# First hop in a bucket pass: gather and scatter runs of four and five without lag, and a PSUM bank moved from the lookup to the gather ring

## The chip, the cores and the metric

One NeuronCore of a Trainium2 chip runs the kernel. The metric is device time in microseconds of one execution. Names used below: TensorE is PE (its weight loads are PEld), VectorE is DVE, ScalarE is ACT, GpSimd is POOL, SyncE is SP, which issues most DMAs. PSUM has eight banks, and a tile here fills a bank or a part of one.

## The reference: what is computed

A graph of 10000 nodes with 160000 random edges and 128 features per node. Seven hops propagate the features over normalized edges; then a small attention block over the eight tokens of every node, and a readout.

```python
h = x
toks = [x]
for _ in range(K):                                   # K = 7
    msg = h[src] * deg_inv_sqrt[src, None] * deg_inv_sqrt[dst, None]
    h = _segment_sum(msg, dst, N)
    toks.append(h)
tok = jnp.stack(toks, axis=1)                        # (N, K+1, D)
t = _layernorm(tok, axis=-1)
...
o = tok + jnp.einsum('nkd,de->nke', o, wo)
...
return jnp.einsum('nk,nkd->nd', alpha, o)
```

## The kernel before, in words

**Stages.** `pass_a` and `decode` sort edges into cells; then comes the bucket pass, which this document is about; hops 2 to 7 follow; attention comes last. Nodes are cut into 79 tiles of 128. The bucket pass handles tiles in quads of four (20 of them), and does three things at once for three quads in a row, as three generators that a loop in `run` advances in turn, sixteen steps per quad:

- `place` (L419) sorts the edges of a quad, two tiles at a time. For each pair it counts keys (L431, 25 matmuls into the PSUM tile `ur`), evicts the counts to `H` (L432, ACT), forms offsets (L437) evicted to `U2` (L439, ACT), ranks by `ux` (L220, DVE) and 16 matmuls L224 and one L225 into `ur` again, reduces the ranks to `rk` (L228, DVE), makes one-hot rows and products `R` (L207, L213, DVE), and looks up with 50 matmuls (L450, 25 for each tile of the pair) into the PSUM tile `tb`, which ACT evicts to `tbs` (L451). `tb` has a bank of its own in the pool `psm`. At a quad's end two DMAs write `srow` and `drow`, small matmuls (L466, L468, L480, L499) make indices and the matrix `Sov` for edges that spill over; `ohp` (L495-L499) are DVE one-hots.
- `matrices` (L509) makes each tile's matrix `w` of gather and scatter one-hots: a row `rb` is loaded (L516), DVE compares it (L525), three matmuls L528 per tile write `x` (PSUM, from the same ring as the gathers, tag "p"), ACT turns `x` into one-hots (L529), DVE adds the rest (L533), and a DMA stores `w` (L535).
- `hop1` (L698) does the first hop for a quad with `block` (L549). A tile has nine gathers. A gather (`gather`, L603) is two passes of four matmuls L609, 32 columns of weights each, into a bank `p` of the ring `pg`; the evacuation to `eb`, one of five buffers, is by ACT (L614), and in the last quad by ACT and DVE in turn. Its scatter (`scat`, L576) is two pairs of matmuls L559 and L560, 128 columns of weights, from `eb` into the accumulator `acc` (two banks). Two fetched rows per tile (`og`, indirect DMAs on POOL, L545) are scattered in the same way; the last of them is in `close` (L589), which ends the tile and hands `acc` to `fin1` (L677: `indeg` on DVE, `y`, `r` and `tab` on ACT and DVE, stores on SP).

**The order in `block`.** `runs` says how many gathers are issued in a row, and `lag` how many scatters stay pending after each run; the rest are emitted behind the run. Then the generator yields. In the first hop runs are 2, 2, 2, 3 with a lag of two, so a scatter is always two gathers behind, and a tile takes four steps. `close` is pending as well, so it comes in the next tile's first run.

**Who orders the queues.** When the program is built, a scheduler sets each engine's order from the program's order, the dependences and its own costs; a queue is then strictly in order. Only attention is ordered by hand.

**PSUM in the bucket pass.** Eight banks: `ur` one, `tb` one, `msc` one, the ring `pg` three, `acc` two.

Of the kernel before, what the change touches and what calls it, by code (L numbers as in the profile page):

```python
# [7 lines left out]
F32 = mybir.dt.float32  # L8
# [7 lines left out]
PSUM = bass.MemoryType.PSUM  # L16
# [14 lines left out]
NS = 4 * NJ  # L31
# [9 lines left out]
class Hops:  # L41
# [377 lines left out]
    def place(self, ts, got):  # L419

        tc, nc, V, A, T, G = self.tc, self.nc, self.nc.vector, self.nc.scalar, self.nc.tensor, self.nc.gpsimd
# [3 lines left out]
        for p0 in range(0, n, 2):  # L425
            cols = lambda z: z[:, :, ts[0] + p0:ts[0] + p0 + 2]
            oh = self.onehot(wp, "oh", cols(self.kB), NS)
            ur = self.pU.tile([128, 512], F32, name="ur")
            H = wp.tile([128, NS, 2], F16, name="H")
            for c in range(NCH):  # L430
                T.matmul(ur[:, :2 * NS], self.id16, oh[:, c], start=c == 0, stop=c == NCH - 1)  # L431
            A.copy(H, ur[:, :2 * NS].rearrange("p (k i) -> p k i", i=2))  # L432
            yield
            U = ur[:, 512 - 2 * NS:].rearrange("p (k i) -> p k i", i=2)
            h = NS // 4
            for w in range(4):
                T.matmul(U[:, w * h:(w + 1) * h], self.triw[:, w, :], H[:, w * h:(w + 1) * h], start=True, stop=True)  # L437
            U2 = wp.tile([128, NS, 2], F16, name="U2")
            A.copy(U2, U)  # L439
            yield  # L440
            rk = self.rank(wp, w1, ur, oh, U2, cols(self.wB))
            ro = self.onehot(w1, "rob", rk, CAP)
            R = w1.tile([128, NCH, 2 * CAP, 2], F16, name="R")
            self.times(R[:, :, :CAP], ro, cols(self.sl))
            self.times(R[:, :, CAP:], ro, cols(self.dl))
            yield
            tb = self.psm.tile([NS, 2, 64], F32, name="tb")
            for g in range(2):
                for c in range(NCH):
                    T.matmul(tb[:, g, :], oh[:, c, :, g], R[:, c, :, g], start=c == 0, stop=c == NCH - 1)  # L450
            A.copy(tbs[:, p0:p0 + 2, :], tb)  # L451
            vo = wp.tile([128, NCH, 2], F32, name="vo")
            V.scalar_tensor_tensor(vo, rk, float(CAP), cols(self.TT), op0=ALU.is_ge, op1=ALU.mult)
            for g in range(2):
                V.max(ov[:, p0 + g, :], vo[:, :, g])
            yield
# [92 lines left out]
    def block(self, t, w, tab, og, pend, lag, runs, first, evac, fin, lead=False, late=False, mid=None, ahead=None,  # L549
              after=None):  # L550

        nc, V, A, T, G = self.nc, self.nc.vector, self.nc.scalar, self.nc.tensor, self.nc.gpsimd
        acc = []

        def both(W, rows, start, ones):

            T.matmul(acc[0][:, :128 + ones], W, rows[:, 128:256 + ones], start=start, stop=False, skip_group_check=True)  # L559
            T.matmul(acc[0][:, :128], W, rows[:, :128], start=False, stop=False, skip_group_check=True)  # L560


        def fetched(i, start=False, stop=False):
            W = w[:, (NG + i) * 128:(NG + i + 1) * 128] if i < NI else self.Sov[:, t, :]
            if first:
                both(W, og[i], False, 0)
                T.matmul(acc[0][:, 128:129], W, self.ones16, start=False, stop=stop, skip_group_check=True)  # L567
                return
            T.matmul(acc[0][:, :256], W, og[i], start=start, stop=stop)  # L569

        def begin():
            acc.append(self.pacc.tile([128, 512], F32, name="acc", tag="acc"))
            for i in range(NI if late else NI + 1):
                fetched(i, start=i == 0)

        def scat(e, jj):  # L576
            if not acc:
                acc.append(self.pacc.tile([128, 512], F32, name="acc", tag="acc"))
            for j in range(e.shape[1]):
                J = 2 * jj + j  # L580
                if first:
                    both(w[:, J * 128:(J + 1) * 128], e[:, j], J == 0, 1)
                else:
                    T.matmul(acc[0][:, :256], w[:, J * 128:(J + 1) * 128], e[:, j, :256], start=False, stop=J == NG - 1 and not late)  # L584
                if first and J == 0 and not lead:
                    for i in range(NI):
                        fetched(i)

        def close():  # L589
            if first:  # L590
                if lead:
                    for i in range(NI):
                        fetched(i)
                fetched(NI, stop=True)
                fin(t, acc[0][:, :128], acc[0])
                return
            if late:
                T.matmul(acc[0][:, :256], self.Sov[:, t, :], og[NI], start=False, stop=True)  # L598
            s = self.fp.tile([128, 128], F32, name="s")
            V.tensor_reduce(s, acc[0][:, 0:256].rearrange("p (h d) -> p d h", h=2), axis=X, op=ALU.add)  # L600
            fin(t, s, acc[0])

        def gather(jj):  # L603
            n = min(2, NG - 2 * jj)
            p = self.pg.tile([128, 2, 2, 128], F32, name="p")
            for j in range(n):
                for q in range(4):
                    s = 4 * (2 * jj + j) + q
                    T.matmul(p[32 * q:32 * q + 32, j], w[:, NJ * 128 + s * CAP:NJ * 128 + (s + 1) * CAP], tab[:, s, :], start=True, stop=True)  # L609
            e = self.ebuf[self.eb_i % len(self.ebuf)]  # L610
            self.eb_i += 1
            pv = p[:, :n].rearrange("p j h d -> p j (h d)")
            if evac(jj):
                A.copy(e[:, :n, 0:256], pv)  # L614
            else:
                V.tensor_tensor(e[:, :n, 0:256], pv, self.one[:, :, None].to_broadcast([128, n, 256]), op=ALU.mult)  # L616
            pend.append(lambda: scat(e[:, :n], jj))

        jj = 0
        for i, n in enumerate(runs):  # L620
            for _ in range(n):
                gather(jj)
                if jj == 0 and not first and not mid:
                    ahead(self.ebuf[(self.eb_i - 1) % len(self.ebuf)][:, 0, 0:1])
                jj += 1
            if mid:
                mid(0)
            if not first:
                begin()
                if mid:  # L630
                    ahead()
            while len(pend) > lag:
                pend.pop(0)()
            if mid:
                mid(1)
            if after:
                after()
            if i == len(runs) - 1:
                pend.append(close)
            yield  # L640
# [17 lines left out]
    def run(self, ctx, att, nhop=K):  # L658
        tc, nc, V, A, T, G = self.tc, self.nc, self.nc.vector, self.nc.scalar, self.nc.tensor, self.nc.gpsimd
        with ExitStack() as c:  # L660
# [3 lines left out]
            self.pass_a()  # L664
            self.decode()
            self.gsp = c.enter_context(tc.tile_pool(name="gs1", bufs=6))
            self.pg = c.enter_context(tc.tile_pool(name="pg1", bufs=3, space=PSUM))
            self.pacc = c.enter_context(tc.tile_pool(name="pc1", bufs=2, space=PSUM))
            self.ogp = c.enter_context(tc.tile_pool(name="og1", bufs=2))
            self.fp = c.enter_context(tc.tile_pool(name="fp1", bufs=1))  # L670
# [1 line left out]
            pend = []  # L672
# [25 lines left out]
            def hop1(q):  # L698
                for t, w in zip(quads[q], W[q]):
                    og = [self.fetch(t, j, (self.tabd[0], self.tabh[0])) for j in range(NI + 1)]  # L700
                    yield from self.block(t, w, self.tab[0], og, pend, 2, (2, 2, 2, 3), True,
                                          lambda jj: q < nq - 1 or jj % 2 == 0, fin1, t == quads[0][0])

            nq, last1 = len(quads), quads[-1][-1]
# [22 lines left out]
        with ExitStack() as c:  # L727
# [10 lines left out]
            pend = []  # L738
            for k in range(2, nhop + 1):
# [30 lines left out]
                og = [[None] * (NI + 1) for _ in order]  # L770
# [11 lines left out]
                for n, t in enumerate(order):  # L782
                    w = self.gsp.tile([128, (NJ + NG) * 128], F8, name="w")
# [546 lines left out]
```

## Time and profile before

| what | value |
|---|---|
| median of 3 runs | 3995.84 us (3982.39 to 4321.17) |
| profiled execution | 4027.3 us, its span 4025.2 us, mean granted TensorE clock 0.974 |
| sorting, until the bucket pass's first gather | 0 to 441 us |
| bucket pass | 441 to 1218 us |
| hops 2 to 7 | 1218 to 3342 us |
| attention | 3342 to 4025 us |

The stages' bounds are the first and last starts of their lines in the trace. The profiled execution is 31 us longer than the median. Busy time is the union of an engine's instructions; matmuls are pipelined and their ends are modelled, so a TensorE that is shown busy may still lose time between instructions, which is seen in their starts.

### The profile page before, as it was taken

How to read it: one execution, taken by the hardware profiler on the slowest of the kernel's cores; microseconds unless marked ns; L12 is line 12 of the kernel's file. 1: busy time of each engine (PE TensorE's matmuls, PEld its weight loads, DVE VectorE, ACT ScalarE, POOL GpSimd, SP SyncE). 2: the span in 40 equal slices, each digit the busy share in tenths (PEclk: the TensorE clock that was granted, in tenths of full speed). 3: DMA queues.
4: the chain of work that ended last, by engine and by line, in shares of the span. 5: the costliest groups of instructions: out<-in, count | busy, mean ns of one | idle time of the engine just before them, and what ended most of it. 6: DMA issues, size and time to landing. Idle time of an engine off the chain costs nothing.

```text
span 4025.2 us, 169111 instructions
## 1 busy us (share of the span) xinstructions
PE 3816.7 (95%) x71507; PEld 3075.5 (76%) x71507; DVE 3203.1 (80%) x6886; ACT 2847.4 (71%) x7067; POOL 1716.4 (43%) x2343
## 2 busy tenths in 40 slices
PE   6887899999999999999999999999999999999997
PEld 4665666667667888888888788888888887887885
DVE  8998777777757777777777777777776665999998
ACT  6884577777776666666666666666665667888884
POOL 0000222232335665666566566656656662222222
PEclk8998899999999999999999999999999999999998
DMA  3100444444455666666666666666666652222220
GB/s 105 31 2 1 146 149 142 146 150 149 149 172 161 198 202 192 202 200 201 193 198 203 188 207 202 200 190 201 202 192 200 187 186 84 74 73 73 78 79 13
DMA packets 326582, 595.67 MB, mean 148 GB/s; under 512 B 61559, under 2 KB 219477, under 8 KB 320565
## 3 DMA queue, kind: packets, MB, share of 16 engines
q1 hardware_dynamic: 287861, 507.11, 40.2%
q0 software_dynamic: 35392, 72.55, 6.4%
q8 instruction: 560, 9.18, 1.0%
q10 hardware_dynamic: 2560, 5.12, 0.4%
q14 instruction: 209, 1.71, 0.1%
HBM read 455.67 MB, written 128.91 MB: 145 GB/s over the span
## 4 chain that ended last, share of the span: by engine, by line
PE 71%; DVE 19%; DMA 5%; ACT 3%; issue 2%; SPq 0%; another core or an unknown queue 0%; DVEq 0%; POOL 0%; POOLq 0%; ACTq 0%
PE p L609 27%; PE acc L584 23%; PE acc L569 4%; DVE o L213 2%; DMA rb<-srow 2%; PE tb L450 2%; PE ur L224 2%; DVE st L1110 2%; DVE oh L207 2%; DVE ux L220 2%; PE acc L559 2%; PE pv L1004 1%; DVE tab L1021 1%; PE po L1015 1%; PE acc L560 1%
## 5 line engine op out<-in xcount | busy, mean ns | idle before, releaser
L614 ACT CAST eb<-p 128x512 f16<-128x512 f32 x3065 | 1623.0, 600 | 562.5 <-PE p L609 336.2
L616 DVE TENSOR_TENSOR eb<-p,one 128x512 f16<-128x512 f32 x1912 | 1232.0, 686 | 328.3 <-PE acc L584 183.6
L609 PE MATMUL p<-tab,w 128*32 128x256 f16 x39816 | 1296.6, 275 | 30.7 <-issue 15.3
L609 PEld LDWEIGHTS <-w 128*32 128x32 fp8e4 x39816 | 989.5, 96 | 233.1 <-issue 177.5
L584 PE MATMUL acc<-eb,w 128*128 128x256 f16 x8532 | 1013.2, 273 | 0.0
L584 PEld LDWEIGHTS <-w 128*128 128x128 fp8e4 x8532 | 836.5, 98 | 98.7
L545 POOL DMA_INDIRECT og<-tabh,oidx x553 | 607.4, 1098 | 675.8 <-DVE vi L490 389.1
L545 POOL DMA_INDIRECT og<-tabd,oidx x541 | 540.9, 1000 | 804.8 <-PE acc L567 453.2
L654 POOL TENSOR_SCALAR r<-s,ctok 128x128 f32<-128x128 f32 x474 | 294.8, 622 | 43.9 <-DVE s L600 27.1
L645 ACT ACTIVATE tab<-s,c 128x128 f16<-128x128 f32 x395 | 158.6, 401 | 206.6 <-DVE eb L616 178.3
L646 DVE SCALAR_TENSOR_TENSOR tab<-s,c,tab 128x128 f16<-128x128 f32 x395 | 138.9, 352 | 180.6 <-issue 169.7
L1029 ACT ACTIVATE junk<-tab 128x128 f32<-128x128 f32 x625 | 245.2, 394 | 0.0
L341 ACT ACTIVATE rs<-iof,rb 128x128 fp8e4<-128x128 f32 x784 | 231.8, 390 | 0.3
L559 PE MATMUL acc<-eb,w 128*128 128x129 f16 x1422 | 215.0, 223 | 1.3 <-ACT eb L614 1.3
L600 DVE TENSOR_REDUCE s<-acc 128x128 f32<-128x256 f32 x474 | 196.8, 415 | 20.2 <-PE acc L598 14.2
L560 PE MATMUL acc<-eb,w 128*128 128x128 f16 x1422 | 210.5, 221 | 0.0
L559 PEld LDWEIGHTS <-w 128*128 128x128 fp8e4 x1501 | 139.0, 98 | 75.9 <-issue 75.9
L529 ACT ACTIVATE w<-x,one 128x512 fp8e4<-128x512 f32 x237 | 149.2, 689 | 62.8 <-PE x L528 60.3
L1015 PEld LDWEIGHTS po<-v,pT 128*128 128x128 f32 x1250 | 159.6, 194 | 42.0 <-issue 27.6
L544 POOL COPY og<-eb 128x1 f16<-128x1 f16 x452 | 83.9, 186 | 250.4 <-ACT eb L614 250.4
L1004 PE MATMUL pv<-Wv,xT 128*128 128x131 f32 x1250 | 176.4, 284 | 1.6 <-ACT xT L984 1.1
L1087 POOL TENSOR_TENSOR p<-e,in 128x512 f32<-128x512 f32 (+1 forms) x40 | 40.8, 1021 | 320.1 <-DVE e L1085 320.1
(301 smaller groups left out, 5448.0 us busy)
## 6 DMA issues: line engine op xcount, KB each, us to landing
w<-gsd SPq DMA_DIRECT2D x474, 592.0 KB
gsd<-w SPq DMA_DIRECT2D x79, 592.0 KB
rb<-srow SPq DMA_DIRECT2D x79, 576.0 KB
tok<-r SPq DMA_DIRECT2D x546, 64.0 KB
tab<-tok SPq DMA_DIRECT2D x273, 128.0 KB
tabd<-tab SPq DMA_DIRECT2D x396, 64.0 KB
og<-tabh,oidx POOLq DMA_INDIRECT x553
og<-tabd,oidx POOLq DMA_INDIRECT x541
```

What stands on the lines that cost most here:

```text
L341: A.activation(ro[:, j - a, i, :], self.iof, AF.Abs_reciprocal_sqrt, scale=2.0 ** 21, bias=rb[:, j - VP, i:i + 1], saturate=False)
L545: self.nc.gpsimd.indirect_dma_start(out=o, out_offset=None, in_=src[0] if i == NI else src[1], in_offset=bass.IndirectOffsetOnAxis(ap=self ...
L559: T.matmul(acc[0][:, :128 + ones], W, rows[:, 128:256 + ones], start=start, stop=False, skip_group_check=True)
L560: T.matmul(acc[0][:, :128], W, rows[:, :128], start=False, stop=False, skip_group_check=True)
L584: T.matmul(acc[0][:, :256], w[:, J * 128:(J + 1) * 128], e[:, j, :256], start=False, stop=J == NG - 1 and not late)
L609: T.matmul(p[32 * q:32 * q + 32, j], w[:, NJ * 128 + s * CAP:NJ * 128 + (s + 1) * CAP], tab[:, s, :], start=True, stop=True)
L614: A.copy(e[:, :n, 0:256], pv)
L616: V.tensor_tensor(e[:, :n, 0:256], pv, self.one[:, :, None].to_broadcast([128, n, 256]), op=ALU.mult)
L654: self.nc.gpsimd.tensor_scalar(r, s, ct[:, t:t + 1], None, op0=ALU.mult)
L1004: T.matmul(p[:, g - a, :], S[i]["xT"][:, g, :], Wv, start=True, stop=True)
L1015: T.matmul(p[:, g - a, :], PT[i % 2][:, g, :], S[i]["v"][:, g, :128], start=True, stop=True)
L1029: A.activation(j, S[i]["x"][:, g, :], AF.Square, bias=S[i]["x"][:, g, 0:1], scale=-1.0, accum_out=S[i]["sq"][:, g:g + 1])
```

## The change

The lookup's tile `tb` becomes a part of `ur`: its columns 256 to 383 of the bank, on the partitions that `tb` used. (The ranks take columns 0 to 249 of `ur`, the offsets 360 to 511, which ACT has copied out before the ranks.) The pool `pg` gets the bank: four instead of three. The first hop runs four and then five gathers, with no lag. In the first hop `block` yields once more in each run, between the gathers and the scatters, so that a tile still takes four steps.

```diff
@@ place
-            tb = self.psm.tile([NS, 2, 64], F32, name="tb")
+            tb = ur[:NS, 256:384].rearrange("p (g v) -> p g v", g=2)
             for g in range(2):
                 for c in range(NCH):
                     T.matmul(tb[:, g, :], oh[:, c, :, g], R[:, c, :, g], start=c == 0, stop=c == NCH - 1)
@@ block
                 begin()
                 if mid:
                     ahead()
+            else:
+                yield
             while len(pend) > lag:
                 pend.pop(0)()
             if mid:
@@ run
-            self.pg = c.enter_context(tc.tile_pool(name="pg1", bufs=3, space=PSUM))
+            self.pg = c.enter_context(tc.tile_pool(name="pg1", bufs=4, space=PSUM))
@@ hop1
-                    yield from self.block(t, w, self.tab[0], og, pend, 2, (2, 2, 2, 3), True,
+                    yield from self.block(t, w, self.tab[0], og, pend, 0, (4, 5), True,
                                           lambda jj: q < nq - 1 or jj % 2 == 0, fin1, t == quads[0][0])
```

## Prediction

> **What bounds the kernel now.** I read the page first, then the busy times by stretch, then the waits of the bucket pass, then the chain in order of time, and last the timelines of three engines over one quad of tiles.
>
> ```profile
> span 4025.2 us, 169111 instructions
> PE 3816.7 (95%) x71507; PEld 3075.5 (76%) x71507; DVE 3203.1 (80%) x6886; ACT 2847.4 (71%) x7067; POOL 1716.4 (43%) x2343
> ```
>
> The change touches only the bucket pass. From the first matmul of hop 2 on, the built programs' TensorE queues are the same instruction by instruction, and so is the whole GpSimd queue but for buffer numbers. The busy times by stretch give the pass its limit (columns: stretch, its length, busy time of PE, PEld, DVE, ACT, POOL, granted clock, DMA share, GB/s).
>
> ```profile
> 700.00:800.00 100.00, 96.98 (x1823) 69.43 (x1820) 78.44 (x132) 76.74 (x165) 28.06 (x20) 1.00 0.43 142
> ...
> 441.00:1160.00 719.00, 694.50 (x12813) 497.08 (x12813) 553.53 (x905) 536.54 (x1148) 205.44 (x141) 0.99 0.45 147
> 441.00:1218.00 777.00, 746.86 (x13809) 532.53 (x13809) 580.00 (x954) 580.91 (x1240) 221.16 (x154) 0.99 0.46 149
> ```
>
> TensorE is busy 97% of the steady pass at full clock; ACT and DVE have about a quarter of it free. The whole pass is 777 us, so 2% of the kernel (80 us) would be 10% of the pass. The waits there (engine, line, what it waited for: us, times, longest) say how little TensorE waits:
>
> ```profile
> ACT eb L614 <- PE p L609: 35.3, 79, 1.1
> ...
> DVE w L525 <- DMA rb<-srow: 18.8, 20, 1.7
> ...
> PE p L609 <- ACT eb L614: 9.6, 30, 0.4
> ...
> PE ur L224 <- DVE ux L220: 8.0, 9, 1.6
> ```
>
> Gathers wait 9.6 us in all for a bank of the three-bank ring, the rank matmuls 8.0 us for DVE. The chain shows the period: a quad is two L450 blocks.
>
> ```profile
> 710.61 1.99 PE tb L450 x50
> ...
> 751.36 1.97 PE tb L450 x50
> ...
> 791.29 1.99 PE tb L450 x50
> ...
> 1153.31 1.97 PE tb L450 x50
> ```
>
> Eleven quads from 710.61 to 1153.31 are 40.25 us each; the one from 751.36 to 791.29, which I walk through below, is a short one (39.93).
>
> **Part 1, fewer changes between gathers and scatters.** G is a gather matmul (L609, eight to a gather of two passes), S a scatter matmul (L559, L560, four to a gather).
>
> ```profile
> 756.53 0.22 PE L559 MATMUL acc<-eb,w 128*128 128x129 f16 x1
> 756.58 0.22 PE L560 MATMUL acc<-eb,w 128*128 128x128 f16 x1
> 756.73 0.62 PE L609 MATMUL p<-tab,w 128*32 128x256 f16 x16
> 757.28 0.23 PE L559 MATMUL acc<-eb,w 128*128 128x129 f16 x1
> ...
> 764.25 0.40 PE L609 MATMUL p<-tab,w 128*32 128x256 f16 x8
> ...
> 781.68 0.85 PE L528 MATMUL x<-diff,dT 5*128 5x512 f16 x3
> 782.47 0.23 PE L559 MATMUL acc<-eb,w 128*128 128x129 f16 x1
> ...
> 750.76 0.60 PE L528 MATMUL x<-diff,dT 5*128 5x512 f16 x2
> ...
> 753.25 0.39 PE L528 MATMUL x<-diff,dT 5*128 5x512 f16 x1
> ```
>
> S to S starts are 0.055 us apart, S to G 0.15: 0.09 extra. Eight more G add 0.62 - 0.40 = 0.22, so sixteen are worth 0.44, yet 756.73 to 757.28 is 0.55: 0.11 extra on the way back. A group of gathers thus costs 0.20 us besides its work. In the built order a steady quad has 25 such groups before and 18 after (not 8, since the scheduler lets gathers of a second run slip between scatters of the first): 7 x 0.20 = 1.4 us less. The three L528 of a tile, together before, stand in single file among scatters in two of four tiles: two more groups net. One more L528 adds 0.60 - 0.39 = 0.21, so three are worth 0.64, and the next scatter follows their start by 0.79 (781.68 to 782.47): 0.15 extra on the way out alone, 0.2 with the way in (estimate): 0.4 us more. Net -1.0 us per quad, -20 us over 79 tiles (19.75 quads), if nothing new waits.
>
> [...]
>
> **Part 2, no lag: a scatter waits for the evictions of its own run.** ACT evicts every gather but in the last quad.
>
> ```profile
> 757.84 0.61 PE L609 MATMUL p<-tab,w 128*32 128x256 f16 x13
> ...
> 760.40 0.56 PE L499 MATMUL msc<-dg,ohp 128*128 128x3 f16 x16
> ```
> ```profile
> 758.42 2.06 ACT L614 CAST eb<-p 128x512 f16<-128x512 f32 x4 [0.59 <-PE p L609]
> ...
> 766.03 0.55 ACT L158 ACTIVATE tab<-y,q 128x256 f16<-128x256 f32 x1
> ...
> 767.38 0.36 ACT L439 CAST U<-ur 128x152 f16<-128x152 f32 x1
> ...
> 777.57 0.26 ACT L451 CAST tbs<-tb 76x128 f16<-76x128 f32 x1 [1.36 <-PE tb L450]
> ...
> 779.35 2.76 ACT L614 CAST eb<-p 128x512 f16<-128x512 f32 x5
> ...
> 787.98 0.59 ACT L614 CAST eb<-p 128x512 f16<-128x512 f32 x1 [0.58 <-PE p L609]
> ```
>
> An eviction starts 0.58 after its gather (757.84 to 758.42), takes 0.59 (787.98), and each next one ends 0.49 later (2.06 for four). The waiting engine goes on about 0.05 after an end (L499 at 760.40, its ohp below done at 760.35). A run of four that nothing covers: 0.58 + 2.06 + 0.05 to be seen + 0.22 for the last four S = 2.9 us; TensorE's own work in it is 4 x 0.22 + 0.11 + 16 x 0.055 + 0.3 for the close and the fetched rows = 2.2. Idle: 0.7. A run of five: the fifth gather needs the first bank back, at 0.58 + 0.59 + 0.05 = 1.2 where four gathers took 0.9, and 0.58 + 2.76 + 0.27 = 3.6 against 5 x 0.22 + 0.11 + 20 x 0.055 = 2.3. Idle: 1.3. Uncovered that is 2.0 per tile, less the switches. Lag two hid it: two older scatters' worth always stood ahead.
>
> What covers it now is the other work between: counts (25 L431, 1.6 us), lookups, L528, L224. I walk the queues of the quad as built, with the rows' durations, against the quad at 751.36.
>
> ```profile
> 757.25 1.23 DVE L207 TENSOR_TENSOR ohp<-ph,io 128x2048 f16<-128x2048 f16 x1
> 759.12 1.23 DVE L207 TENSOR_TENSOR ohp<-ph,io 128x2048 f16<-128x2048 f16 x1 [0.65 <-PE msc L499]
> 760.26 1.42 DVE L525 TENSOR_SCALAR w<-rb,pid 128x2304 fp8e4<-128x2304 f16 x1
> ...
> 767.77 2.14 DVE L220 TENSOR_TENSOR ux<-oh,U 128x3800 f16<-128x3800 f16 x1
> ...
> 772.11 0.42 DVE L228 TENSOR_REDUCE rk<-ur 128x50 f16<-128x250 f32 x1 [2.20 <-PE ur L225]
> ```
>
> - First tile: its run of four idles about 0.6 and the fifth gather 0.3, but both orders then stand before the second L499 block, which needs the second ohp (759.12 + 1.23 = 760.35). The DVE order up to it is the same. Net 0; what the fewer groups save is lost there too.
> - Second tile: first scatter 0.4 late behind its eviction, which is queued on ACT behind three L529; gathers of the run of five slip between the scatters and hide the rest; two more L528 groups. Its tab (L158) and U (L439) now stand behind four evictions, not two: ux starts 0.6 later than 767.77, and L224 is covered. Net +0.25.
> - Third tile: 32 G and straight its scatters, idle 0.7; 40 G, idle 0.3 at the fifth bank; one L525 has moved between rk and rob on DVE (1.3 more in the chain to L450), of which 0.15 shows. Less three groups saved. Net +0.45.
> - Fourth tile: 0.5 at the first scatter, 0.35 at the fifth bank, 0.4 at the last two evictions; less a group or two. Net +0.6.
>
> Sum +1.3 against a quad of 39.93. Against the mean of 40.25 it is about 1.0: long quads lose their 0.3 to a late rb row, which holds L525 and through it ux, and ux now has 0.6 of slack behind tab. Between 1.0 and 1.3 I take 1.1 per quad; twenty quads, the ramp and the last ones at the same price: **+22 us**.
>
> **Part 3, tb in the rank bank.** The next count (L431) into ur must now wait for tbs. In one of two pairs per quad the count comes some 8 us after L450: nothing. In the other it followed at once, and even began before L450; now six S (0.33) cover the 0.26 us of tbs and its start: 0.13 left, in the third tile's sum. Bounds: nothing, and 0.26 + 0.1 at both pairs, 14 us in all. **Four banks** give back at most the 9.6 us above; the fifth gather of a run takes that again, as counted.
>
> **Part 4, fetches.** A tile's indirect DMAs wait for the close of the tile two before; the close comes two gathers (0.44 us) later.
>
> ```profile
> L545 POOL DMA_INDIRECT og<-tabh,oidx x71 | 115.4, 1626 | 97.9 <-PE acc L567 35.3 <-PE acc L560 34.7 <-DVE tab L159 22.1
> ```
>
> An issue takes 1.6 us and the row is needed a whole tile (10 us) later: nothing; without that cover, 0.44 x 79 = 35 us. On SP, the loads of rb move past single gsd or tok writes; rb is needed one to two tiles on, and what is at stake are the 18.8 us that L525 waits now.
>
> **Sum.** +22: -20 from the groups, so that exposed evictions, the tbs wait and the DVE chain cost about 42. The profiled execution took 4027.3 (span 4025.2), so 4049 by its own time; it lies 31 us over the median of the runs, 3995.84. I predict 3995.84 + 22 = 4018.
>
> **Rivals.** (a) The covers hold better than I walk it, and only the groups count: -20, 3976, faster, though by less than 2%. It decides if the evictions after a run are done before TensorE arrives, that is if idle per tile stays under 0.25. For it: ACT is free a quarter of the time. Against it: three runs of a quad have nothing between gathers and scatters. (b) The covers do not hold: ACT's queue keeps L529, y, r and tab ahead of evictions, and every run idles 2.0 less 0.4 for two groups: 1.6 x 79 = 126 us, 4122. Half of that, 1.0 per tile, is already slower by 2%. For it: ACT's strict order. Against it: half of a quad's TensorE time is other work, some of it between. [...] (c) The DVE chain rk, L525, rob, R before L450 becomes the bound: 1.3 more in one of two pairs, 26 us more than my sum, 4044. For it: L525 also waits for rb. Against it: 0.15 is all that shows by the walk.
>
> **Chances.** My forecast with (c): 0.57. (a): 0.26. (b): 0.15. Anything else 0.02. The range reaches from (a), with a few us for part 3 and the clock, 3970, to 4080, which leaves out most of (b). The forecast's own range is 4003 to 4045. A change under 2% is about what a measurement of this kernel can tell from none (runs from 3982.39 to 4321.17). Faster by over 2% has 0.02, since the groups give 20 us at most; slower by over 2% most of (b), 0.13; within 2% the rest, 0.85.
>
> **What would show it.** Waits of L559 for ACT eb should be 15 to 40 us in the pass, and L609's wait for eb some 10 to 20; L224's wait for ux should shrink. L450 blocks should stand 41.3 us apart by quads. ACT's wait for p should rise above 35.3. Rows after hop 2's start must not change in length. Wrong would be: quads under 40.2 (a) or above 43 (b), or L450 waiting over 1 us for R (c).

## The result and the profile after

The changed kernel takes 4034.48 us (median of 4 runs, 4031.47 to 4035.49); the kernel before, run beside it, 3995.89. The ratio is 1.0107 [1.0081, 1.0132]: slower, by less than 2%, with the whole interval above 1. It compares the means of the fast runs; one of the four runs of the kernel before, at 4321.17, was slow and is not in it. The profiled execution took 4031.47, its span first on the page:

```profile
span 4029.4 us, 169173 instructions
PE 3812.7 (95%) x71507; PEld 3097.5 (77%) x71507; DVE 3189.8 (79%) x6886; ACT 2796.2 (69%) x7067; POOL 1692.9 (42%) x2343
```

This span is only 4 us above that of before, since the later hops ran faster in this execution. The busy times by stretch show it (columns as in the prediction). First hops 2 to 7, from their first scatter to their last, in the kernel after, together with the ramp (the sorting of the first quads, ahead of the first gathers) and a steady stretch:

```profile
1259.00:3348.00 2089.00, 2077.63 (x43557) 1760.30 (x43555) 1588.01 (x3244) 1361.38 (x2761) 1307.25 (x1873) 1.00 0.65 198
...
375.00:463.00 88.00, 58.02 (x569) 44.67 (x566) 59.60 (x89) 14.55 (x35) 5.98 (x4) 0.62 0.22 66
...
700.00:800.00 100.00, 97.06 (x1724) 70.55 (x1725) 74.34 (x119) 72.67 (x158) 23.57 (x20) 1.00 0.48 154
```

The same view of the kernel before:

```profile
1228.00:3343.00 2115.00, 2092.34 (x43554) 1762.34 (x43553) 1602.70 (x3243) 1402.14 (x2760) 1305.06 (x1867) 1.00 0.64 196
...
375.00:463.00 88.00, 71.08 (x946) 53.19 (x945) 71.72 (x108) 31.49 (x71) 11.88 (x8) 0.77 0.32 102
```

Hops 2 to 7 have the same TensorE queue in both kernels and differ by 26 us. By the experiments this goes with the chip and not with the kernel: the first four, on one chip, took 2089 to 2096 there, all later ones, on three others, 2118 to 2122, whatever they did in the pass. The kernel before itself took 3987 (median) on the chip of the first four, and 4029 to 4033 on the three others. So spans are not subtracted here; the pass is read from its own starts, and whole times only as ratios. Hop 1 ends (last L567) at 1217.4 before and at 1254.7 after, 37 us later; the ratio stands for 43 [32, 53].

Where the 37 us arise is read from the starts of the L450 blocks. The sixth, when hop 1 has just begun, in the timeline of before:

```profile
467.03 2.02 PE L450 MATMUL tb<-R,oh 128*76 128x64 f16 x50
```

In the timeline of after the sixth starts 23.5 us later, and the rows behind it give the steady quads:

```profile
490.54 2.00 PE L450 MATMUL ur<-R,oh 128*76 128x64 f16 x50 [0.35 <-DVE R L213]
...
737.10 2.05 PE L450 MATMUL ur<-R,oh 128*76 128x64 f16 x50
...
778.36 2.05 PE L450 MATMUL ur<-R,oh 128*76 128x64 f16 x50
...
1190.90 2.05 PE L450 MATMUL ur<-R,oh 128*76 128x64 f16 x50
```

So 23 us are lost in the ramp, before the pass runs steadily. Eleven quads in 453.80 (737.10 to 1190.90) are 41.25 each, against 40.25 before: 11 us more over these eleven, and 14 over the seventeen quads from the sixth L450 on. The tail, from the last L450 to the end of hop 1, is the same (64.2 before, 63.8 after).

The ramp row tells the other half: TensorE is busy 58 of 88 us, not 71, at a granted clock of 0.62, not 0.77. The timeline of the kernel before there (start, duration, engine, line; in brackets idle before and what ended it):

```profile
388.20 2.07 PE L431 MATMUL ur<-oh,id 128*128 128x152 f16 x25 [0.51 <-DVE rk L228]
...
391.16 2.02 PE L450 MATMUL tb<-R,oh 128*76 128x64 f16 x50 [0.26 <-DVE R L213]
393.45 1.86 PE L224 MATMUL ur<-ux,id 128*128 128x250 f16 x16 [0.27 <-DVE ux L220]
...
395.86 1.81 PE L431 MATMUL ur<-oh,id 128*128 128x152 f16 x25 [0.30 <-DVE rk L228]
...
398.82 2.01 PE L450 MATMUL tb<-R,oh 128*76 128x64 f16 x50 [0.47 <-DVE R L213]
```

and of the kernel after:

```profile
392.41 3.48 PE L450 MATMUL ur<-R,oh 128*76 128x64 f16 x50 [3.46 <-DVE R L213]
...
395.92 0.26 ACT L451 CAST tbs<-ur 76x128 f16<-76x128 f32 x1 [12.43 <-PE ur L450]
...
396.23 3.02 PE L431 MATMUL ur<-oh,id 128*128 128x152 f16 x25 [0.35 <-ACT tbs L451]
...
402.43 3.32 PE L224 MATMUL ur<-ux,id 128*128 128x250 f16 x16 [2.54 <-DVE ux L220]
...
409.25 3.48 PE L450 MATMUL ur<-R,oh 128*76 128x64 f16 x50 [3.46 <-DVE R L213]
```

Before, the next pair's count (L431) goes into `ur` as soon as the ranks are out of it, and runs while DVE makes the rows of this pair's lookup. After, the bank stays with the pair through the ranks, L450 and `tbs`, so the next count waits for all of it. There is no hop work yet to fill the time, and a pair takes 16.84 us (392.41 to 409.25) where it took 7.66 (391.16 to 398.82). Of the 9.2 us, 4.1 are the lower clock: the same L450, L431 and L224 take 3.48, 3.02 and 3.32, not 2.02, 1.81 and 1.86. The other 5.1 come from work that now stands in line.

The waits of the steady pass (after, 463 to 1190) show little of the steady loss:

```profile
ACT eb L614 <- PE p L609: 74.1, 70, 1.8
...
DVE w L525 <- DMA rb<-srow: 35.9, 31, 2.3
...
PE ur L450 <- DVE R L213: 2.3, 5, 0.8
```

ACT waits twice as long for gathers as before (35.3). TensorE's scatters have no row of waiting for ACT's `eb`, and the gathers (L609) wait only 0.4 for it:

```profile
L609 PE MATMUL p<-tab,w 128*32 128x256 f16 x5040 | 222.0, 277 | 6.4 <-ACT eb L614 0.4 <-ACT w L529 0.2
```

The starts show it. A run of four in the timeline of TensorE (after, third tile of the quad from 778.36):

```profile
799.92 1.06 PE L609 MATMUL p<-tab,w 128*32 128x256 f16 x32
...
801.37 0.22 PE L560 MATMUL acc<-eb,w 128*128 128x128 f16 x1
801.56 0.22 PE L559 MATMUL acc<-eb,w 128*128 128x129 f16 x1
...
801.72 0.22 PE L560 MATMUL acc<-eb,w 128*128 128x128 f16 x1
802.05 0.22 PE L559 MATMUL acc<-eb,w 128*128 128x129 f16 x1
...
802.21 0.22 PE L560 MATMUL acc<-eb,w 128*128 128x128 f16 x1
802.54 0.22 PE L559 MATMUL acc<-eb,w 128*128 128x129 f16 x1
...
802.85 1.55 PE L609 MATMUL p<-tab,w 128*32 128x256 f16 x40
```

The scatters of its last three gathers start 0.49 us apart (801.56, 802.05, 802.54), the pace of ACT's evictions (2.05 us for the four from 800.43, so 0.49 for each behind a first of 0.59). Between them stand starts 0.33 apart, not 0.055, but the profile models a matmul as 0.22 long, so only 0.11 looks idle, and nothing is put down to a releaser. The run of five after it: x40 in 1.55, and x32 in 1.06, so its last eight took 0.49, not 0.22.

### The profile page after: what moved, and what is told of

It reads as the page before. It is cut to its first block, busy times and chain, and to the rows that moved or that the text cites. A ratio compares the mean times of both kernels' runs of the same rounds, so it can differ in the third digit from the quotient of the medians.

```text
span 4029.4 us, 169173 instructions
## 1 busy us (share of the span) xinstructions
PE 3812.7 (95%) x71507; PEld 3097.5 (77%) x71507; DVE 3189.8 (79%) x6886; ACT 2796.2 (69%) x7067; POOL 1692.9 (42%) x2343
## 5 line engine op out<-in xcount | busy, mean ns | idle before, releaser
L614 ACT CAST eb<-p 128x512 f16<-128x512 f32 x3065 | 1567.3, 609 | 597.7 <-PE p L609 594.6
L616 DVE TENSOR_TENSOR eb<-p,one 128x512 f16<-128x512 f32 x1912 | 1190.3, 684 | 312.0 <-PE p L609 310.7
L609 PE MATMUL p<-tab,w 128*32 128x256 f16 x39816 | 1274.2, 274 | 11.6 <-ACT eb L614 3.2
L609 PEld LDWEIGHTS <-w 128*32 128x32 fp8e4 x39816 | 1007.0, 96 | 211.8 <-issue 154.3
L545 POOL DMA_INDIRECT og<-tabh,oidx x553 | 581.2, 1051 | 661.7 <-DVE oidx L471 400.7
L648 DVE SCALAR_TENSOR_TENSOR tab<-s,c,tab 128x128 f16<-128x128 f32 x395 | 163.6, 414 | 180.5 <-ACT tab L647 180.5
L559 PE MATMUL acc<-eb,w 128*128 128x129 f16 x1422 | 229.3, 222 | 9.6
L560 PE MATMUL acc<-eb,w 128*128 128x128 f16 x1422 | 222.5, 219 | 0.0
L559 PEld LDWEIGHTS <-w 128*128 128x128 fp8e4 x1501 | 140.9, 97 | 49.8 <-issue 41.3
L1017 PE MATMUL po<-v,pT 128*128 128x128 f32 x1250 | 166.6, 277 | 7.0 <-DVE tab L1023 5.4
```

What stands on the lines that cost most here:

```text
L545: self.nc.gpsimd.indirect_dma_start(out=o, out_offset=None, in_=src[0] if i == NI else src[1], in_offset=bass.IndirectOffsetOnAxis(ap=self ...
L1017: T.matmul(p[:, g - a, :], PT[i % 2][:, g, :], S[i]["v"][:, g, :128], start=True, stop=True)
```

## Experiments

Theory A: there are two separate costs, the ramp (+23 us, by `tb` in the rank bank alone) and about +1.0 us per steady quad (by the runs without lag, whose scatters and fifth gathers wait for ACT's evictions). Rival B: the shared bank costs in the steady quads too, and the runs nothing. Rival C: behind the long runs something else than evictions sets the quad (DVE's chain of counts, ranks and lookups). In the table, hop 1's times and the steady quad (mean of the last eleven, from the first and last L450) are of each kernel's profiled execution; "groups" are runs of gathers without another matmul between, per quad. By this count before has 26 and after 19. Ratios are to the kernel before on the same chip.

| kernel | runs, lag | `tb` | ring | ratio | first gather | hop 1 ends | quad | groups |
|---|---|---|---|---|---|---|---|---|
| before | 2, 2, 2, 3, lag 2 | own | 3 | 1 | 441.3 | 1217.4 | 40.25 | 26 |
| after | 4, 5, lag 0 | `ur` | 4 | 1.0107 [1.0081, 1.0132] | 463.5 | 1254.7 | 41.25 | 19 |
| e1_share_only | as before | `ur` | 3 | 1.0075 [1.0058, 1.0092] | 463.6 | 1244.0 | 40.45 | 28 |
| e2_runs_only | 4, 5, lag 0 | own | 3 | 1.0097 [1.0080, 1.0114] | 440.2 | 1252.6 | 42.33 | 20 |
| e3_ramp_acc | 4, 5, lag 0 | `acc`, then `ur` | 4 | 1.0055 [1.0039, 1.0072] | 439.0 | 1233.0 | 41.14 | 19 |
| e4_share_bank | as before | `ur` | 4 | 1.0043 [1.0026, 1.0059] | 461.4 | 1228.2 | 40.04 | 21 |
| e5_lag2_bank_ramp | as before | `acc`, then `ur` | 4 | 0.9980 [0.9971, 0.9989] | 439.5 | 1206.2 | 39.73 | 21 |
| e6_dve_evicts | as e3 | as e3 | 4 | 1.0068 [1.0053, 1.0082] | 441.9 | 1251.5 | 42.06 | 18 |
| e9_lag1_six | 4, 5, lag 1 | as e3 | 4 | 1.0023 [1.0013, 1.0033] | 437.1 | 1227.1 | 40.98 | 18 |
| e10_lag2_seven | 4, 5, lag 2 | as e3 | 4 | 1.0075 [1.0061, 1.0088] | 436.1 | 1245.6 | 42.42 | 27 |
| e11_half_45 | as e3, half evictions | as e3 | 4 | 1.0021 [1.0009, 1.0034] | 437.3 | 1219.1 | 40.85 | 15 |
| e12_half_2223 | as e5, half evictions | as e5 | 4 | 0.9973 [0.9961, 0.9985] | 439.7 | 1203.1 | 39.64 | 20 |

Two cautions for reading it. Hop 1's end is that of one execution and the ratio that of many, and the two differ by up to 7 us (e3: 16 us later than before by hop 1, 22 by the ratio). And a few of the quads ran at a granted clock of 0.96 and were 1.5 to 3.4 us longer than the others: one of the eleven in e1, three in e2, two in e4, two in e12. Without them the means are 40.16 (e1), 41.94 (e2), 39.65 (e4) and 39.29 (e12); in the other rows all eleven were at full clock.

**e1: before, with tb in ur.**

```diff
-            tb = self.psm.tile([NS, 2, 64], F32, name="tb")
+            tb = ur[:NS, 256:384].rearrange("p (g v) -> p g v", g=2)
```

> The lookup in the rank bank alone: runs 2, 2, 2, 3, lag two and three banks as before. Theory A (two costs: the ramp of the first two quads runs in a row, since the next count waits until the lookup of the pair before is out of the bank, 23 us; and 1.0 us per steady quad by exposed evictions, 14 us): the first gather comes 20 to 24 us later than before's 441, steady quads stay within 40.0 to 40.6, the time is 18 to 24 us over before. Theory B (the missing lag makes all of it): the first gather within 5 us of 441 and no change of time. Theory C (the shared bank costs in the steady pass as well): quads of 41 or more and over 35 us more.

The first gather comes 22 us late, as in after, and the ramp row is after's again (kernel e1, by stretch and by timeline):

```profile
375.00:463.00 88.00, 57.65 (x575) 44.51 (x572) 60.69 (x92) 14.83 (x35) 5.98 (x4) 0.65 0.21 66
```
```profile
409.80 3.48 PE L450 MATMUL ur<-R,oh 128*76 128x64 f16 x50 [3.46 <-DVE R L213]
```

Nine of the last eleven quads are 40.02 to 40.26 long, so the bank is nearly free there: B falls in its first half. Hop 1 ends 26.6 us late, and the time is 30 us over before, more than the 18 to 24 expected. Two neighbouring quads of 44.7 and 43.4 are 8 us of that. The granted clock was 0.92 and 0.96 there, with half speed shortly after a long wait for DVE's `ux` in each. The first wait, and the busy times by stretch just behind it (clock third from the end):

```profile
710.87 2.92 PE L224 MATMUL ur<-ux,id 128*128 128x250 f16 x16 [1.74 <-DVE ux L220]
```
```profile
711.40:714.80 3.40, 3.40 (x20) 1.84 (x22) 0.90 (x2) 0.40 (x1) 0.00 (x0) 0.50 0.06 22
```

**e2: the runs alone.** After, with `tb` in a tile of its own and so three banks.

```diff
-            tb = ur[:NS, 256:384].rearrange("p (g v) -> p g v", g=2)
+            tb = self.psm.tile([NS, 2, 64], F32, name="tb")
...
-            self.pg = c.enter_context(tc.tile_pool(name="pg1", bufs=4, space=PSUM))
+            self.pg = c.enter_context(tc.tile_pool(name="pg1", bufs=3, space=PSUM))
```

> Runs of four and five without lag alone: the lookup in its own bank, so the ring has three banks and the fourth gather of a run waits for an eviction as the fifth did. Theory A: the first gather at 441 to 446, steady quads of 41.2 to 43, the time 15 to 50 us over before, all of it after 500 us. Theory B: 35 us or more, of which 20 before the first steady quad. Theory C: quads under 40.6.

The ramp is whole (first gather at 440.2), and the quads are 2.1 us longer than before (1.7 without the three at the lower clock), all of the loss in the steady pass: the runs cost, and B falls in its second half too. With four banks the same comparison, e3 against e5 below, gives 1.4.

**e3: after, without the ramp's loss.** In the first two quads there is no hop work and the accumulators are idle, so the lookup writes there.

```diff
-            tb = ur[:NS, 256:384].rearrange("p (g v) -> p g v", g=2)
+            tb = (self.pacc.tile([128, 512], F32, name="tb", tag="acc")[:NS, 256:384] if ts[0] >= 4 * NG else ur[:NS, 256:384]).rearrange("p (g v) -> p g v", g=2)
```

> The changed kernel, but in the first two quads, when no hop runs yet, the lookup is in one of the two accumulator banks; steady queues are the changed kernel's. Theory A: the first gather back at 441 to 446, steady quads of 41.1 to 41.4 as in the changed kernel, and 18 to 24 us less than the changed kernel, 12 to 20 over before. Theories B and C: within 5 us of the changed kernel.

```profile
375.00:463.00 88.00, 68.17 (x963) 50.26 (x963) 71.84 (x107) 31.32 (x70) 13.66 (x8) 0.84 0.32 102
```
```profile
714.90 2.03 PE L450 MATMUL ur<-R,oh 128*76 128x64 f16 x50
...
1167.40 2.05 PE L450 MATMUL ur<-R,oh 128*76 128x64 f16 x50
```

TensorE's busy time in the ramp is back near that of before, hop 1 ends 22 us earlier than in after, and the quads keep their 41.14 (452.50 / 11). Moving the tile in two quads of twenty takes the whole ramp cost away and nothing else. A holds on both counts so far, though the time, 22 us over before, is a little above the 12 to 20 expected.

**e4: the four banks, with the old runs.** e1 with `bufs=4`.

> The lookup in the rank bank and four banks in the ring, but runs 2, 2, 2, 3 and lag two. The built order has 21 groups of gathers in a steady quad where before has 25 and the changed kernel 18. Theory A: the ramp's 20 to 24 us are lost, steady quads come to 39.4 to 40.2 (four groups at 0.20 us and what is left of waits for a bank), so 5 to 22 us over before. Theory B: no loss at all, 5 to 15 us faster than before. Theory C: quads of 41 or more.

The ramp is lost again (461.4), and the quads are 40.04, their shortest 39.49 where e1's is 40.02. The groups of gathers fall from 28 to 21: with a fourth bank the scheduler itself joins gathers, with the runs unchanged.

**e5: e4 with e3's line**, that is without the ramp's loss.

> Runs 2, 2, 2, 3 and lag two as before, the lookup in the rank bank, four banks in the ring, and the first two quads' lookup in an accumulator bank. Theory A adds up: the ramp of before (first gather at 439 to 442), steady quads of 39.5 as with shared bank and four banks, so hop 1 ends 10 to 13 us earlier than before's 1217 and the time is 8 to 14 us (0.2 to 0.35%) under before. If the gains do not add up, the time is within 4 us of before.

```profile
705.57 2.03 PE L450 MATMUL ur<-R,oh 128*76 128x64 f16 x50
...
1142.59 2.03 PE L450 MATMUL ur<-R,oh 128*76 128x64 f16 x50
```

The quads are 39.73 (437.02 / 11), hop 1 ends 11 us earlier than before, and the kernel is 0.2% faster than before: the best version found that does all the work.

**e6: DVE takes two of a tile's nine evictions.** e3, and the last gather of each run goes to DVE.

```diff
-                                           lambda jj: q < nq - 1 or jj % 2 == 0, fin1, t == quads[0][0])
+                                           lambda jj: jj not in (3, 8) if q < nq - 1 else jj % 2 == 0, fin1, t == quads[0][0])
```

> The changed kernel with the ramp mended, and the last gather of each run is evicted by DVE in place of ACT. If evictions exposed on ACT make the steady quads 41.13, two engines shorten the end of each run by about 0.4 us, eight runs a quad, partly covered: 39.8 to 40.8. If DVE's queue, with 2.1 us instructions in order, is worse than ACT's: 41.5 to 43. If the order of TensorE alone sets it, 41.0 to 41.3.

```profile
700.00:1100.00 400.00, 374.58 (x6875) 276.75 (x6874) 343.99 (x557) 250.74 (x539) 102.10 (x76) 1.00 0.42 141
```

It is slower, 42.06 a quad. ACT's busy time falls, DVE's rises to 344 of 400 us, and TensorE's falls to 375. Its rows of waits for `eb` in this stretch come to 9.0 us, 3.9 for DVE's and 5.1 for ACT's, where e3 has none; over 9.5 quads that is about the 0.9 a quad that was lost. DVE's queue also carries the lookup chain, so evictions stand behind it there; that this is why they came late was not tested.

**e7: e3 with lag 1 and five buffers**, and **e8: e3 without the extra yield.**

```diff
-                    yield from self.block(t, w, self.tab[0], og, pend, 0, (4, 5), True,
+                    yield from self.block(t, w, self.tab[0], og, pend, 1, (4, 5), True,
```
```diff
-            else:
-                yield
```

> The changed kernel with the ramp mended, runs of four and five but a lag of one: one gather's scatters stand ahead in every run. The built order has 15 groups of gathers a quad (18 without lag). Theory A: each run's wait falls by the 0.22 us of the older scatters and three groups give 0.6 us more, so quads of 39.6 to 40.6. Rival, that the lag is not what counts: 41.0 to 41.3 less the 0.6 at most, 40.5 or more, with waits of evictions for gathers as long as without lag.

> The changed kernel with the ramp mended and without the new yield between the gathers and scatters of a run: a tile takes two steps and nothing is emitted between them, though the built order still lets parts of the lookup slip in. Theory A: more of the 0.7 and 1.3 us of uncovered run shows: quads of 41.5 to 44. Rival, that the place of the yield does not count: 41.0 to 41.3.

e7 (1.0174 [1.0159, 1.0189], quads of 43.5 to 44.9) does not test the lag. With five buffers the fifth gather of the run of five takes the buffer of the gather still pending, so one scatter per tile waits for the run's last eviction and reads another gather's rows. e9 does it with six buffers. e8 took 4309.41 in its single execution, with quads of 54 to 58, far above the 41.5 to 44 expected: by the code a tile then takes two steps and not four, so that half of a quad's steps have no hop work. The granted clock from 700 to 1100 was 0.81, which could make up to 10 of the 13 us and more (estimate: 41.14 / 0.81 = 50.8); the rest was not taken apart. Without the yield the change would have cost far more.

**e9: lag 1 with six buffers.** e3's four banks and `tb` line, lag 1, and room for the sixth buffer from two tiles that are needed early only.

```diff
-        self.more_ebufs(cp, 5)
+        self.more_ebufs(cp, 6)
...
-                    yield from self.block(t, w, self.tab[0], og, pend, 0, (4, 5), True,
+                    yield from self.block(t, w, self.tab[0], og, pend, 1, (4, 5), True,
```

> Runs of four and five with the ramp mended and a lag of one, with a sixth buffer behind the evictions so that a pending scatter still reads its own gather (two tables that are used only at the start give up the space). Theory A, that the wait for a run's own evictions is what the steady quads pay: 39.6 to 40.6 a quad against 41.13 without lag, so 10 to 28 us less than the changed kernel with the ramp mended. Rival, that it is the order and the number of pieces: 40.9 to 41.3.

40.98 a quad, only 0.16 less than without lag. If evictions alone held the quad, a lag should have given back most of a microsecond. The waits from 700 to 1100 (line numbers here are three higher; L453 is the lookup, L502 the `msc` product) now name DVE:

```profile
PE msc L502 <- DVE ohp L210: 5.6, 10, 0.6
...
PE ur L453 <- DVE R L216: 4.0, 9, 0.4
...
PE p L612 <- ACT eb L617: 2.5, 12, 0.4
```

**e10: lag 2 with seven buffers** (and five, not six, in the pool `gs1` to make room).

> Runs of four and five with the ramp mended and a lag of two, as before, with seven buffers behind the evictions; the ring of gather and scatter matrices gives up one of six for the space. Theory A: with the lag of before no run waits for its own evictions, and quads are at or under the 39.5 of runs 2, 2, 2, 3 with four banks: 38.8 to 39.8, the time 8 to 24 us under before. Rival, that the scheduler cuts the runs up again (the built order shows 24 groups of gathers where lag none had 18), so that the longer runs bring nothing: 39.5 to 40.2. If the five matrices run short, DVE waits for scatters at L525 and L533 over 20 us in the pass and quads are over 40.3.

Slower, 42.42. With two scatters pending the scheduler cuts the runs up again: 27 groups. Eight more than e3 at 0.20 each would be 1.6 (estimate from the switch price), and the quad is 1.3 longer. The other sign, DVE waiting over 20 us in the pass for scatters before it may write the next matrix (L525 and L533), came true as well, with 24.4 us. But e3 has 18.1 at L525 with six matrices, and L450 waited for `R` only 1.3 us in e10's pass, so it is not seen to reach TensorE. Other causes were not excluded.

**e11: half evictions with the new runs, and e12: the same with e5.** Each eviction in hop 1 copies half of its bank; the other half of `eb` keeps old values.

```diff
-                A.copy(e[:, :n, 0:256], pv)
+                A.copy(e[:, :n, 0:128] if first else e[:, :n, 0:256], p[:, :n, 0] if first else pv)
```

> The changed kernel with the ramp mended, and ACT copies only the upper half of each gather of the first hop (128 columns of 256 per pass; the lower halves, the residuals, are left out, so their scatters add the buffer's old contents). Evictions take about 0.35 us, one after another 0.27. If evictions that a run waits for make the steady quads (theory A), all such waits go, and with 15 groups of gathers a quad, quads are 37.8 to 39.0. If DVE's lookup chain or the order sets the quads whatever ACT does: 40.4 to 41.1.

> The same halved evictions under runs 2, 2, 2, 3 with lag two, four banks and the mended ramp (the lower halves left out as well). TensorE's order is that of the full evictions but for a few pieces (20 groups of gathers). Theory A: evictions were hidden here already, so quads go from 39.57 to 38.9 to 39.5 only, and the long runs with halved evictions are the faster of the two by 0.5 to 1.2 a quad. If DVE's chain sets the quads: 39.4 to 39.6 here and the long runs stay slower.

e11's quad is 40.85, only 0.29 under e3's, and e12's 39.64 against e5's 39.73 (39.29 without the two at the lower clock). Halving the evictions thus leaves the gap between the two orders about as it was: 1.41 with whole evictions (e3 and e5), 1.21 or, at full clock, 1.56 with half ones. First e3, then e11 with three of its waits, all from 700 to 1100:

```profile
700.00:1100.00 400.00, 389.11 (x7068) 287.57 (x7067) 306.80 (x500) 290.18 (x632) 98.71 (x78) 1.00 0.43 143
```
```profile
700.00:1100.00 400.00, 365.93 (x7086) 282.85 (x7086) 313.24 (x505) 225.54 (x637) 116.77 (x80) 1.00 0.46 147
```
```profile
PE ur L450 <- DVE R L213: 14.6, 19, 2.0
...
PE msc L499 <- DVE ohp L207: 7.0, 10, 0.7
PE ur L224 <- DVE ux L220: 5.2, 10, 1.3
```

ACT's busy time falls by 64.6 us, some 0.18 for each of about 350 evictions (estimate: 9.8 quads of 36), where a whole one took 0.49 in a row: an eviction of half a bank is shorter, but by this not by half. TensorE loses 23 us of busy time, and 26.8 us of waits for DVE appear, 2.7 for each of the 9.8 quads in the stretch; e3 has none of the three there. So in the new order whole evictions end the waits first, and what they hid is C: by these waits DVE's chain through `ux`, `ohp` and `R` keeps the quads at 40.3 or more even where an eviction copies half. No run shortened that chain, so that it is the bound is read from the waits and not tested. The order of two and three gathers ran at 39.5 with full evictions. The part of A that the evictions alone make the microsecond falls; its forecast that with half evictions the long runs would be the faster, by 0.5 to 1.2 a quad, came out the other way.

## Why the prediction was right, and where it was wrong

The time, 4034, lies in the range and in the forecast's own range (4003 to 4045); the direction was right, and the size was about half: +22 predicted, 39 by the medians and 43 by the ratio. It is in part luck that it lies there: of the 37 us in hop 1, the 23 of the ramp came from a term that the sum put at nothing, and the steady pass cost 14, not 22.

**Part 1, the groups: the count right, the price open.** It counted 25 and 18 in the built order; the traces have 26 and 19 by the table's count. The 0.20 for a group was not measured by itself. e4 has seven groups fewer than e1, 1.4 us by that price, and is only 0.4 shorter (0.5 at full clock), a fourth bank included; e10 has eight more than e3 and is 1.3 longer. That the walked quad came out is no test of the price, since a smaller gain and a smaller loss add up to the same.

**Part 2, the evictions: the quad right to 0.1 us, the cause right as far as it went.** Predicted quads of 41.3, measured 41.25. The sum charged 1.1 to all twenty quads, 22 us; from the sixth L450 to the last, seventeen quads, it was 14.2 (700.4 against 686.2), and the tail paid nothing. The pieces can be seen: a bare run of four idles 0.7, by the starts of 801.37 to 802.54 above (0.19 + 0.33 + 0.33 less 3 x 0.055 = 0.69); the fifth bank costs 0.3, measured 0.49 - 0.22 = 0.27. What the sum did not say, and e9 and e11 show, is that a second limit stands just behind: even with half of each eviction copied the quad stays at 40.85, far from the 39.25 of rival (a).

**Part 3, tb in the rank bank: the step that failed.** It priced the wait for `tbs` in the steady quad, 0.13 us, with 14 us as the bound from above, and took "the ramp and the last ones at the same price". In the steady quad that is so: in after the count that follows a lookup starts 0.23 us behind the scatter before it (806.66 to 806.89). In the ramp nothing covers the chain, and it cost 22 to 23 us by e1 and e3, as much as the whole forecast and above the bound. The bound was made from the eviction's length (0.26), though what a shared bank holds up is everything from the ranks to `tbs`: 7.7 us became 16.8 in the first pair. The row that would have told it was in the kernel before: L431 at 388.20 starts ahead of L450 at 391.16, with no hop work near either. The fall of the clock nearly doubled the price (4.1 beside 5.1 us in the first pair).

**Four banks: half right.** "At most 9.6 us" fits the old runs: e1 to e4 gains 0.4 a quad (0.5 at full clock), 8 to 10 us. With the new runs the fourth bank is worth 1.2 a quad (e2 to e3, 42.33 to 41.14), or 0.8 at full clock; the walk had runs and bank together, so its total does not depend on that.

**Part 4, fetches: right in effect.** L525's wait for `rb` rose from 18.8 to 35.9, but L450 waits for `R`, which stands behind it on DVE, 2.3 us in all.

**The rivals.** (a) and (b) are out by the quad, 41.25. (c) is out for the change as it is, with 2.3 us of waits of L450 for `R` in the whole pass and none above 0.8, and comes true once the evictions are shortened (e11, 14.6 us in 400).

**What would show it.** Right: the quads, ACT's wait for `p` above 35.3 (74.1), and L224's wait for `ux`, which shrank from 8.0 to no row at all. Wrong: the waits of L559 for `eb`, predicted at 15 to 40, have no row, and L609's is 0.4, not 10 to 20, since a wait that ends before the modelled end of the matmul ahead of it is not shown. Wrong also: the rows of hops 2 to 7 did change in length, by the chip and not by the change.

## What to carry to other kernels

Before two tiles share a PSUM bank, look for the stretch where the engine has no other work, above all the first and last rounds of a pipeline, and walk the whole chain that holds the bank there, not only the eviction that frees it. Before lengthening runs of one kind of matmul, ask what stands in line behind a whole run: here DVE's lookups, so that by the waits the gain from fewer changes of kind was gone even where evictions copied half. A fourth bank let the scheduler join gathers with no new runs (26 to 21 groups a quad), and that alone, with the ramp mended, beat both kernels. And look at the granted clock of each round before comparing means: a few quads at 0.96 made up a third of the difference between e2 and e3, and hid most of what e12 gained on e5.

## What the runs showed of the hardware that was not expected

**The granted clock in a pipeline's start.** Bursts of 3.0 to 3.5 us of matmuls between idle stretches of 2.5 to 3.5 us ran at half clock (0.50 to 0.57 in the rows below): 50 L450 took 3.48 us, not 2.02. In after L450 and the count behind it are busy for 6.5 us with 0.35 idle between, and the count still runs slowly (3.02 for 25). The busy times by stretch of after over that L450, the count, and the later L224 (the clock is third from the end):

```profile
392.40:395.90 3.50, 3.48 (x50) 3.37 (x50) 0.14 (x2) 0.00 (x0) 0.00 (x0) 0.50 0.00 0
395.90:399.30 3.40, 3.07 (x41) 2.94 (x40) 2.14 (x1) 0.27 (x2) 0.00 (x0) 0.57 0.03 5
402.40:405.80 3.40, 3.36 (x17) 2.37 (x17) 0.00 (x0) 0.00 (x0) 0.00 (x0) 0.52 0.00 0
```

The slow L450 stands behind 3.46 us of idle time, the slow L224 behind 2.54. The slow count, at 0.57 in the second row, shows that the clock was not yet back after the 3.48 busy us of L450; whether its gap of 0.35 mattered is open.

**The clock falls behind still shorter gaps in the steady pass, but not always.** L224's wait of 1.74 us for `ux` in e1 (710.87) was followed by half clock (0.50 from 711.40 to 714.80), and so were waits of 1.36 to 2.08 us at L224 in e4 and e12. In e2 the clock fell to 0.50 at 796.9, though TensorE had been busy for 8.1 of the 8.8 us before by the profile. In e11 L450 waited 1.97 us for `R` (896.23), and the clock stayed at 1.00. So in these runs the length of one gap does not decide it; what does stays open.

**The same queue at two speeds.** Hops 2 to 7 took 2089 to 2096 us in after and in the first four experiments, and 2115 to 2122 in the execution of before and on the three other chips. A part of it is seen at hop 2's start, where gathers come in groups of four with an idle time that nothing releases. Before:

```profile
1220.35 0.32 PE L609 MATMUL p<-tab,w 128*32 128x256 f16 x4 [0.30 <-issue]
1221.07 0.34 PE L609 MATMUL p<-tab,w 128*32 128x256 f16 x4 [0.40 <-issue]
```

After, all 72 in one row:

```profile
1256.15 2.25 PE L609 MATMUL p<-tab,w 128*32 128x256 f16 x72 [1.28 <-ACT r L654]
```

What makes the issue slower there stays open.
